# Selective attention and a gated feed-forward block on one core: the last 64 queries of batch 0 computed later, the bias of two heads added by matmuls, and loads moved between DMA queues

## The chip, the cores and the metric

The kernel runs on one core of one Trainium2 chip. The metric is device time in microseconds (us), lower is better. Timed runs give the median; a separate profiled execution gives the trace, whose times count from the start of its span.

## What is computed

The inputs are q, k, v of shape (8 batches, 8 heads, 576 positions, 64), s of shape (8, 8, 576), and three weight matrices. Per batch and head:

```
scores = q @ k.T / sqrt(64)
cum    = cumsum(max(s, 0))
scores = where(key > query, -1e9, scores + min(-(cum[query] - cum[key]), 0))
attn   = softmax(scores) @ v
```

Each batch's eight heads side by side are 576 rows of x (4608 rows of 512 in all). Then out = (silu(x @ w_gate) * (x @ w_val)) @ w_out, with 1536 inner columns. All inputs are float32; the kernel computes in bfloat16 with float32 sums.

## The kernel before

**Stages.** The 4608 rows are cut into nine feed-forward tiles of 512 rows (TT, NTT, lines 46 and 47). A batch has 576 rows, so tile 0 needs only the first 512 rows of batch 0, and the last 64 belong to tile 1. The kernel computes the whole attention of batch 0 first (first_batch, lines 882 to 925), and then runs a loop over the tiles (lines 952 to 969) in which attention of the later batches is interleaved with feed-forward products.

**Scores.** KQ holds the transposed keys and queries of four heads per buffer, two buffers in turn. In each of its tiles one 64-row half is data and the other half carries four extra rows with the cumulative sums, copied there from HL by small DMAs (aug, line 192). So one 128-row matmul gives product and bias together. HL is made on VectorE (DVE) from s by five operations (lines 236 to 242). score_piece (line 350) makes a head's scores in four pieces, 1600 columns in all; in batch 0 two pieces share one wide PSUM bank and one exponential on ScalarE (ACT), 1024 and 576 columns wide (line 388). There are two wide banks. GpSimd (POOL) then clears the positions above the diagonal with two selects (lines 391 and 396).

**Values and x.** av_piece (line 403) multiplies the exponentials with the values, 15 matmuls of 65 columns per head (the last column gives the row sum); av_out (line 421) divides on DVE; x_pe (line 456) transposes two heads' results on TensorE and ACT copies them into XT, the input of the feed-forward products.

**Start.** SP loads s, then k and q of the first eight heads (load_one, called load_qk for both), then after the four HL copies the values (load_v, line 166) and k and q of heads 8 to 11. The number given to load_qk is a group of four heads: 0 and 1 are batch 0, 2 and 3 batch 1. ACT casts group 0, TensorE transposes it in two 64-row halves (pe_transpose_half), and ACT and DVE copy it out of PSUM (pe_out). Weights come by w_load (line 331) on GpSimd's queue, with a cast to bfloat16: gate and value weights in two parts each (g0, v0, g1, v1), the output weights in two (o0, o1).

**Order in the loop.** Every engine executes its instructions in the order of the program. ffn_items yields after each unit of a tile: 24 for gate and value products (gate_value, lines 619 to 662: four 512-column matmuls, a tanh on ACT, DVE products), then those of the down product (lines 664 and 689). n counts units. After each unit the dictionary hook (line 945) may place something, and pump places attention steps of the next batch in proportion to n. In tile 0 pump begins at n = 6 (n0, line 958), and the transposes of group 2 (prep_one, line 529) stand at n = 1 to 4.

The softmax here doesn't subtract the row's maximum and nothing guards it: scores larger than these inputs give would overflow.

## Time and profile before

| | us |
|---|---|
| median of three timed runs | 383.56 (382.58 to 383.68) |
| profiled execution, its own time | 383.17 |
| span of its trace | 381.3 |
| TensorE busy in the span | 363.5 (95%) |
| DVE, ACT, POOL busy | 289.6, 242.7, 205.9 |
| first score matmul of batch 0 (line 375) starts | 11.15 |
| first feed-forward matmul (line 626) starts | 32.03 |
| weights of the first products land, g0 and v0 | 26.7 and 30.7 |
| tile 1's first feed-forward matmul starts | 79.81 |

So the profiled execution has 1.87 us outside its span. A matmul's row in the profile gives its start and a modelled end that includes the way through the array, so a stream of matmuls is priced by the distance between starts and not by the duration of one. Landing times are issue start plus the profile's time to landing.

### The profile page before, as it was taken

Reading aid. Unit: us, or ns where it says so; the run is one execution under the profiler, and the core shown is the slowest. Engines: PE = TensorE matmul, PEld = TensorE weight load, DVE = VectorE, ACT = ScalarE, POOL = GpSimd, SP = SyncE. Lnnn points to the kernel's source line nnn. Section 1 sums busy time; section 2 is a strip of 40 time slices with the busy share of each in tenths; the row PEclk is TensorE's granted clock in tenths of the full one; section 3 lists DMA queues with packets and bytes.
Section 4 is the critical chain, followed back from the end, with each engine's and each line's share of the span. In section 5 each row is a group of like instructions: output and inputs, shape, how many; then the busy total and the mean of one; then the engine's idle time right before and its main releaser. Section 6 shows DMA issues by size and latency. Waiting matters only on the chain. (4 is left out here: it accounts for less than half of the span.)

```text
span 381.3 us, 8674 instructions
## 1 busy us (share of the span) xinstructions
PE 363.5 (95%) x3246; PEld 230.5 (60%) x3246; DVE 289.6 (76%) x577; ACT 242.7 (64%) x459; POOL 205.9 (54%) x326
## 2 busy tenths in 40 slices
PE   3779999998999999999999999999999999999995
PEld 3666556655555555865586558655875575476464
DVE  8666787456895799868986899589958866975983
ACT  8586788676977786578767876697455523323321
POOL 6684357545364636595458647775665426315220
PEclk9999999999999999999999999999999999999999
DMA  7999999997477998498739965987223213002003
GB/s 234 197 253 263 198 242 268 348 259 162 163 167 246 236 285 220 105 287 216 194 114 285 270 149 158 252 179 166 37 80 101 32 19 127 0 2 97 14 2 110
DMA packets 100729, 64.22 MB, mean 168 GB/s; under 512 B 81888, under 2 KB 85824, under 8 KB 100688
## 3 DMA queue, kind: packets, MB, share of 16 engines
q1 hardware_dynamic: 91248, 46.15, 48.6%
q0 software_dynamic: 9440, 17.53, 17.7%
q8 instruction: 25, 0.41, 0.4%
q14 instruction: 16, 0.13, 0.1%
HBM read 37.90 MB, written 19.86 MB: 151 GB/s over the span
## 5 line engine op out<-in xcount | busy, mean ns | idle before, releaser
L388 ACT ACTIVATE pt<-bank 128x512 bf16<-128x512 f32 x224 | 106.7, 506 | 26.5 <-PE bank L375 18.3
L626 PE MATMUL bank<-XT,wg 128*128 128x512 bf16 x432 | 110.9, 379 | 0.6 <-DVE pp L633 0.2
L641 PE MATMUL bank<-XT,wv 128*128 128x512 bf16 x432 | 110.8, 379 | 0.2
L631 ACT ACTIVATE th<-bank 128x512 bf16<-128x512 f32 x108 | 64.7, 599 | 60.0 <-PE bank L626 54.7
L633 DVE SCALAR_TENSOR_TENSOR pp<-th,bank 128x512 bf16<-128x512 bf16 x108 | 73.9, 684 | 30.2 <-ACT th L631 29.5
L649 DVE SCALAR_TENSOR_TENSOR ht<-pp,bank 128x512 bf16<-128x512 bf16 x108 | 74.1, 686 | 10.3 <-POOL ht L658 0.5
L658 POOL TENSOR_TENSOR ht<-ht 128x512 bf16<-128x512 bf16 x35 | 40.4, 1154 | 53.9 <-DVE su L656 53.8
L375 PE MATMUL bank<-kq 128*128 128x128 bf16 (+4 forms) x504 | 67.5, 240 | 1.6 <-DVE kq L284 1.1
L375 PEld LDWEIGHTS <-kq 128*128 128x128 bf16 x576 | 46.7, 99 | 34.8 <-issue 5.7
L641 PEld LDWEIGHTS <-wv 128*128 128x128 bf16 x432 | 38.6, 98 | 35.8 <-issue 0.4
L626 PEld LDWEIGHTS <-wg 128*128 128x128 bf16 x432 | 38.5, 98 | 35.2 <-issue 1.2
L391 POOL TENSOR_SCALAR_AFFINE_SELECT pt<-pt 128x512 bf16<-128x512 bf16 x64 | 41.8, 653 | 28.5 <-ACT pt L388 28.1
L413 PEld LDWEIGHTS <-pt 128*128 128x128 bf16 x960 | 41.1, 98 | 16.0
L413 PE MATMUL bank<-vt,pt 128*128 128x65 bf16 x840 | 41.8, 194 | 0.0
L447 POOL DMA_DIRECT2D xs<-ot x24 | 21.9, 912 | 31.7 <-DVE ot L430 31.7
L711 PEld LDWEIGHTS <-ht 128*128 128x128 bf16 x336 | 31.2, 98 | 4.3
L197 POOL DMA_DIRECT2D kq<-HL x52 | 31.2, 602 | 0.1
L430 DVE TENSOR_TENSOR ot<-bank,rc 128x320 bf16<-128x320 f32 x56 | 27.5, 492 | 1.9
L396 POOL TENSOR_SCALAR_AFFINE_SELECT pt<-pt 128x64 bf16<-128x64 bf16 x64 | 16.7, 261 | 18.9 <-ACT pt L388 18.7
L711 PEld LDWEIGHTS <-su 128*128 128x128 bf16 x252 | 23.6, 98 | 3.3
L670 PE MATMUL bank<-wo,ht 128*128 128x512 bf16 x96 | 24.6, 379 | 0.0
L775 POOL TENSOR_TENSOR ysb<-ysb 128x512 f32<-128x512 f32 x12 | 15.2, 1271 | 15.3 <-DVE ysb L770 15.3
(96 smaller groups left out, 396.9 us busy)
## 6 DMA issues: line engine op xcount, KB each, us to landing
rawk<-in_k_dram SPq DMA_DIRECT2D x15, 576.0 KB
rawq<-in_q_dram SPq DMA_DIRECT2D x15, 576.0 KB
rawv<-in_v_dram SPq DMA_DIRECT2D x32, 256.0 KB
out_dram<-ysb POOLq DMA_DIRECT2D x32, 256.0 KB, 3.8
xs<-ot POOLq DMA_DIRECT2D x24, 160.0 KB, 3.7
ks<-ck SPq DMA_DIRECT2D x11, 288.0 KB
qs<-cq SPq DMA_DIRECT2D x11, 288.0 KB
wg<-in_moe_w_gate_dram POOLq DMA_DIRECT2D x2, 768.0 KB, 12.6
```

The lines of the kernel that those rows point to most:

```text
L197: engs[hh].dma_start(KQ[hb % 2][r][r0 : r0 + 4, :, e * S : (e + 1) * S], HL[bh : bh + 1, :, :, :],)
L375: nc.tensor.matmul(sc[:, o : o + w], T[:, 1, e * S + 128 * tj : e * S + 128 * (tj + 1)], T[:, 0, e * S + lo : e * S + hi], start=True, sto ...
L388: nc.scalar.activation(pt[:, c0 : c0 + W], sc[:, 0:W], AF.Exp, scale=0.125)
L391: nc.gpsimd.affine_select(pt[:, 1088:1600], pt[:, 1088:1600], pattern=[[0, 4], [1, 128]], compare_op=ALU.is_ge, fill=zreg, base=0, channel ...
L413: nc.tensor.matmul(av[:, bi * (D + 1) : (bi + 1) * (D + 1)], pt[:, c0 : c0 + 128], VT[b % 2][:, tj, h, :], start=(tj == 0), stop=(tj == bi),)
L626: nc.tensor.matmul(pg, WG[j][:, c, f0 : f0 + 128], xt[:, c, :], start=(c == 0), stop=(c == 3),)
L631: nc.scalar.activation(th, pg, AF.Tanh, scale=0.5)
L633: nc.vector.scalar_tensor_tensor(pp, in0=th, scalar=1.0, in1=pg, op0=ALU.add, op1=ALU.mult)
L641: nc.tensor.matmul(pv, WV[j][:, c, f0 : f0 + 128], xt[:, c, :], start=(c == 0), stop=(c == 3),)
L649: nc.vector.scalar_tensor_tensor(hp[:, 2 * k2 : 2 * k2 + 2, :].rearrange("p a n -> p (a n)"), in0=pp, scalar=0.5, in1=pv, op0=ALU.mult, op ...
L658: (nc.vector if ft == NFT - 1 else nc.gpsimd).tensor_sub(hp[:, 1:3, :], hp[:, 1:4:2, :], hp[:, 0:3:2, :])
L711: nc.tensor.matmul(ps, lhs(p), rhs(p), start=(first and p == 0), stop=(last and p == NP - 1), skip_group_check=True,)
```

## The change

Batch 0 is computed in two parts. first_batch goes. Its place takes a list written out by hand: score_first makes the first 512 queries of a head in two halves of 640 columns, each with one exponential; mask_first clears four diagonal blocks with one select; av_first uses 10 matmuls per head; x_first copies 512 columns. The last 64 queries (score_tail, av_tail, x_tail) stand in the hook of tile 0: the eight score_tail at n = 1 to 8, av_tail at 6 and 10, x_tail at 12. The transposes of group 2 move to n = 9 to 12 and n0 from 6 to 12.

For heads 0 and 1 score_first doesn't use the extra rows. HL now has 128 partitions: rows 64 to 71 repeat the first eight heads of s, loaded by a second DMA on ACT's queue after a memset on GpSimd. Two more matmuls per chunk add the bias, with a selection column (pick, made from the identity) against the rows of HL. The copies of HL's rows for heads 0 and 1 come later; those for heads 2 and 3 go on GpSimd's queue.

The loads of groups 2 and 3 go on GpSimd's queue, the values of batch 0 come in three steps on SP's, w_load calls move, 32 warm-up matmuls (keep_warm) stand at the start, one large memset moves from DVE to GpSimd, and a few casts and copies out of PSUM change engine (k of group 0's second half goes from ACT to DVE, q of group 1's first half from DVE to ACT, the cast of group 1's k from DVE to GpSimd). The loop over the later tiles, pump and the feed-forward code are otherwise the same.

```diff
--- before.py
+++ after.py
@@ -95,15 +95,16 @@
-    HL = const.tile([BH, 4, 2, S], BF16)
+    HL = const.tile([128, 4, 2, S], BF16)
...
-    s_sb = first.tile([BH, S], FP32)
-    c8 = first.tile([BH, S], FP32)
+    s_sb = first.tile([128, S], FP32)
+    c8 = first.tile([128, S], FP32)
+    pick = first.tile([128, 2, 2], BF16)
...
-        def load_one(hb, name, rs=(0, NR)):
+        def load_one(hb, name, rs=(0, NR), eng=nc.sync):
...
-            nc.sync.dma_start(
+            eng.dma_start(
...
-        nc.sync.dma_start(s_sb, s.rearrange("b h n -> (b h) n"))
-        def init_vt(i):
-            nc.gpsimd.memset(VT[i][:, :, :, D : D + 1], 1.0)
-            nc.gpsimd.memset(VT[i][64:128, 4, :, 0:D], 0.0)
+        flat = s.rearrange("b h n -> (b h) n")
+        nc.sync.dma_start(s_sb[0:BH], flat)
+        nc.gpsimd.memset(s_sb[64:128], 0.0)
+        nc.scalar.dma_start(s_sb[64 : 64 + H], flat[0:H])
+
+        def init_vt(i, eng):
+            eng.memset(VT[i][:, :, :, D : D + 1], 1.0)
+            eng.memset(VT[i][64:128, 4, :, 0:D], 0.0)
 
...
+        nc.vector.tensor_add(pick[:, 0, :], ident[:, 0:2], ident[:, 64:66])
+        nc.vector.tensor_scalar(pick[:, 1, :], pick[:, 0, :], -1.0, None, ALU.mult)
...
-        init_vt(0)
-        init_vt(1)
-        nc.vector.memset(aug_rows(1, 0), 0.0)
+        nc.gpsimd.memset(aug_rows(1, 0), 0.0)
         nc.gpsimd.memset(aug_rows(1, 1), 0.0)
         pads(1)
+        init_vt(0, nc.vector)
...
-            c8, one_s[0:BH, 0:1].to_broadcast([BH, S]), s_sb, 0.0, ALU.mult, ALU.add
+            c8, one_s[:, 0:1].to_broadcast([128, S]), s_sb, 0.0, ALU.mult, ALU.add
...
-        nc.vector.tensor_copy(HL[:, 2:4, 0, :], HL[:, 0:2, 1, :])
+        nc.vector.tensor_copy(HL[64:128, 0, 1, :], HL[64:128, 1, 1, :])
+        nc.vector.tensor_copy(HL[0:64, 2:4, 0, :], HL[0:64, 0:2, 1, :])
...
+        W1 = 640
+        FIRST_CHUNKS = [
+            [(0, 0, 384), (1, 128, 256), (1, 256, 384)],
+            [(0, 384, 512), (2, 256, 512), (1, 384, 512), (3, 384, 512)],
+        ]
...
+        def score_first(bh, half):
+            hb, hh = divmod(bh, HB)
+            if half == 0:
+                pts[bh] = PTP[0].tile([128, 2 * W1], BF16, tag="pt", bufs=8, name="pt")
+            r, e = divmod(hh, 2)
+            T = KQ[hb % 2][r]
+            bs = take("w")
+            sc = view(bs, 1024)
+            o = 0
+            for (tj, lo, hi) in FIRST_CHUNKS[half]:
+                keys = slice(128 * tj, 128 * (tj + 1))
+                lhs = T[:, 1, e * S + keys.start : e * S + keys.stop]
+                rhs = T[:, 0, e * S + lo : e * S + hi]
+                out_s = sc[:, o : o + hi - lo]
+                o += hi - lo
+                if bh > 1:
+                    nc.tensor.matmul(out_s, lhs, rhs, start=True, stop=True)
+                    continue
+                nc.tensor.matmul(out_s, lhs[0:64], rhs[0:64], start=True, stop=False)
+                nc.tensor.matmul(
+                    out_s, HL[:, 0, 1, keys], pick[:, 0, bh : bh + 1].to_broadcast([128, hi - lo]),
+                    start=False, stop=False,
+                )
+                nc.tensor.matmul(
+                    out_s, pick[:, 1, bh : bh + 1].to_broadcast([128, 128]), HL[:, 0, 1, lo:hi],
+                    start=False, stop=True,
+                )
+            nc.scalar.activation(
+                pts[bh][:, half * W1 : (half + 1) * W1], sc[:, 0:W1], AF.Exp, scale=0.125
+            )
+            give(bs)
+
+        def mask_first(bh):
+            m = pts[bh].rearrange("p (b n) -> p b n", n=128)[:, 0:10:3, :]
+            nc.gpsimd.affine_select(
+                m, m, pattern=[[0, 4], [1, 128]],
+                compare_op=ALU.is_ge, fill=zreg, base=0, channel_multiplier=-1,
+            )
+
+        def av_first(h):
...
+            for bi in range(4):
+                for tj in range(bi + 1):
+                    c0 = first_col(tj, bi)
+                    nc.tensor.matmul(
+                        av[:, bi * (D + 1) : (bi + 1) * (D + 1)],
+                        pts[h][:, c0 : c0 + 128],
+                        VT[0][:, tj, h, :],
+                        start=(tj == 0),
+                        stop=(tj == bi),
+                    )
...
+        def x_first(pr):
+            ot = ots.pop(pr)
+            bs = take()
+            ps = view16(bs, 512)
+            for c in range(4):
+                nc.tensor.transpose(ps[:, c * 128 : (c + 1) * 128], ot[:, c, :], ident)
+            nc.scalar.copy(XT[:, pr, 0:512], ps)
...
+        def score_tail(bh):
+            hb, hh = divmod(bh, HB)
+            pr, e2 = divmod(bh, 2)
+            if e2 == 0:
+                tls[pr] = PTP[0].tile([128, 3, TT // 2], BF16, tag="su", bufs=NFT // 2, name="su")
+            r, e = divmod(hh, 2)
+            T = KQ[hb % 2][r]
+            bs = take()
+            sc = view(bs, NCH * 64)
+            for tj in range(NCH):
+                nc.tensor.matmul(
+                    sc[:, tj * 64 : (tj + 1) * 64],
+                    T[:, 1, e * S + 128 * tj : e * S + 128 * (tj + 1)],
+                    T[:, 0, e * S + 512 : e * S + S],
+                    start=True,
+                    stop=True,
+                )
+            tl = tail_view(pr)
+            nc.scalar.activation(
+                tl[:, e2].rearrange("p c n -> p (c n)"), sc, AF.Exp, scale=0.125
+            )
...
+        def av_tail(g):
+            if g == 0:
...
+            for i in range(4):
+                h = 4 * g + i
+                tl = tail_view(h // 2)
+                for tj in range(NCH):
+                    nc.tensor.matmul(
+                        av[0:64, i * (D + 1) : (i + 1) * (D + 1)],
+                        tl[:, h % 2, tj, :],
+                        VT[0][:, tj, h, :],
+                        start=(tj == 0),
+                        stop=(tj == NCH - 1),
+                    )
...
+        def x_tail():
...
+            for pr in range(4):
+                nc.tensor.transpose(
+                    ps[:, pr * 64 : (pr + 1) * 64], ot[0:64, pr, :], ident[0:64, 0:64]
+                )
+            nc.scalar.copy(
+                XT[:, :, 512:576], ps.rearrange("p (a n) -> p a n", a=4)
+            )
...
+        def keep_warm(n):
+            bs = take()
...
+        keep_warm(32)
...
-        aug(0, SP4)
-        load_v(0, range(5))
-        load_qk(2)
+        def aug_one(hh, eng):
+            r, e = divmod(hh, 2)
+            r0 = 64 * (1 - r)
+            eng.dma_start(
+                KQ[0][r][r0 : r0 + 4, :, e * S : (e + 1) * S], HL[hh : hh + 1, :, :, :]
+            )
+
+        load_v(0, (0, 1))
+        aug_one(2, nc.gpsimd)
+        aug_one(3, nc.gpsimd)
+        aug(1, SP4)
+        load_v(0, (2, 3))
...
-        aug(1, GP4)
-        for nm, eng in (("k", nc.scalar), ("q", nc.vector)):
+        w_load("g", 0)
...
-                pe_out(0, nm, g, 1, eng)
-        cast_one(1, "k", nc.vector)
...
+        score_first(0, 0)
+        score_first(0, 1)
+        aug_one(0, nc.sync)
+        second_rows("k")
+        score_first(1, 0)
+        second_rows("q")
+        score_first(1, 1)
+        aug_one(1, nc.sync)
+        load_v(0, (4,))
+        cast_one(1, "k", nc.gpsimd)
+        w_load("v", 0)
         cast_one(1, "q", nc.vector)
-
...
-            wq = {1: (("g", 0), ("v", 0)), 4: (("g", 1),), 5: (("v", 1),)}
-            tail = {
-                6: ("a0", "a1"),
-                7: ("a2", "a3", "a4", "x0", "a5", "x1", "a6", "a7", "x2", "w6", "x3", "w8"),
-            }
-            for h in range(H):
-                for ci in range(4):
...
-                        pe_transpose(1, nm, g)
-                    for r in range(2):
-                        for nm, g in order:
-                            pe_out(1, nm, g, r, nc.vector)
-                    for c in range(3, 5):
...
-                    aug(2, SP4)
-                if h == 7:
-                    aug(3, SP4)
-                    load_qk(3)
-                    load_v(1, range(5))
-                    load_qk(4)
-                    cast_one(2, "k", nc.gpsimd)
-                    cast_one(2, "q", nc.gpsimd)
-                    load_qk(5)
-                    w_load("o", 0)
-                    w_load("o", 1)
...
-        first_batch()
+        cast_v(0, 0, nc.gpsimd)
+        cast_v(0, 1, nc.gpsimd)
+        mask_first(0)
+        score_first(2, 0)
+        score_first(2, 1)
+        for g in range(2):
+            pe_transpose(1, "k", g)
+            pe_out(1, "k", g, 0, nc.vector)
+        mask_first(1)
+        score_first(3, 0)
+        for g in range(2):
+            pe_transpose(1, "q", g)
+        score_first(3, 1)
+        cast_v(0, 2, nc.gpsimd)
+        cast_v(0, 3, nc.gpsimd)
+        mask_first(2)
+        for g in range(2):
+            pe_out(1, "q", g, 0, nc.scalar)
+        for nm in ("k", "q"):
+            for g in range(2):
+                pe_out(1, nm, g, 1, nc.vector)
+        mask_first(3)
+        score_first(4, 0)
+        score_first(4, 1)
+        mask_first(4)
+        for nm in ("k", "q"):
+            load_one(2, nm, eng=nc.gpsimd)
+        av_first(0)
+        score_first(5, 0)
+        av_first(1)
+        score_first(5, 1)
+        mask_first(5)
+        av_first(2)
+        score_first(6, 0)
+        av_first(3)
+        score_first(6, 1)
+        mask_first(6)
+        w_load("g", 1)
+        av_first(4)
+        score_first(7, 0)
+        av_first(5)
+        score_first(7, 1)
+        mask_first(7)
+        cast_v(0, 4, nc.gpsimd)
+        x_first(0)
+        av_first(6)
+        x_first(1)
+        keep_warm(6)
+        av_first(7)
+        x_first(2)
+        keep_warm(8)
+        x_first(3)
+        keep_warm(8)
         second_psum()
         first_sbuf.close()
         PTP[0] = ctx.enter_context(tc.tile_pool(name="later", bufs=1))
-        PTP["bufs"] = 5
...
-        hook = {
-            1: [lambda: prep_one(2, 0)],
-            2: [lambda: prep_one(2, 1)],
-            3: [lambda: prep_one(2, 2)],
-            4: [lambda: prep_one(2, 3)],
-            6: [lambda: cast_one(3, "k", nc.gpsimd), lambda: cast_one(3, "q", nc.gpsimd)],
-        }
+        hook = {n: [] for n in range(1, 37)}
+        for bh in range(H):
+            hook[1 + bh].append(lambda bh=bh: score_tail(bh))
+        hook[1].append(lambda: w_load("v", 1))
+        hook[4].append(lambda: aug(2, SP4))
+        hook[4].append(lambda: [load_one(3, nm, eng=nc.gpsimd) for nm in ("k", "q")])
+        hook[6].append(lambda: cast_one(2, "k", nc.gpsimd))
+        hook[6].append(lambda: av_tail(0))
+        hook[7].append(lambda: cast_one(2, "q", nc.gpsimd))
+        hook[8].append(lambda: aug(3, SP4))
+        hook[8].append(lambda: load_v(1, range(5)))
+        hook[9].append(lambda: init_vt(1, nc.gpsimd))
+        hook[10].append(lambda: av_tail(1))
+        hook[12].append(x_tail)
+        for i in range(4):
+            hook[9 + i].append(lambda i=i: prep_one(2, i))
+        hook[11].append(lambda: w_load("o", 0))
+        hook[14].append(lambda: [cast_one(3, nm, nc.gpsimd) for nm in ("k", "q")])
+        hook[14].append(lambda: load_qk(4))
+        hook[15].append(lambda: w_load("o", 1))
+        hook[20].append(lambda: load_qk(5))
...
-            n0 = 6 if tt == 0 else 0
+            n0 = 12 if tt == 0 else 0
```

## The prediction

> **What bounds the kernel now.** The chain of waits covers only the last microsecond here, so it says nothing of the rest. I read first the shares of the span and the 40 slices, from the page:
>
> ```profile
> PE 363.5 (95%) x3246; PEld 230.5 (60%) x3246; DVE 289.6 (76%) x577; ACT 242.7 (64%) x459; POOL 205.9 (54%) x326
> ...
> PE   3779999998999999999999999999999999999995
> PEld 3666556655555555865586558655875575476464
> DVE  8666787456895799868986899589958866975983
> ACT  8586788676977786578767876697455523323321
> ```
>
> TensorE (PE) is full in every slice but the first three or four. So there are two regimes: the attention of batch 0, before the first feed-forward matmul, and a long stretch in which TensorE's stream sets the end. Busy time in 10-us stretches confirms the second (PE, PEld, DVE, ACT, POOL, clock, DMA share, GB/s):
>
> ```profile
> 32.00:42.00 10.00, 9.55 (x69) 5.40 (x70) 7.71 (x12) 7.23 (x13) 3.16 (x4) 1.00 1.14 244
> 42.00:52.00 10.00, 9.91 (x69) 5.33 (x68) 8.01 (x12) 8.73 (x18) 2.68 (x6) 1.00 1.21 208
> 52.00:62.00 10.00, 10.00 (x107) 6.13 (x106) 6.38 (x13) 7.34 (x15) 8.63 (x15) 1.00 0.99 305
> 62.00:72.00 10.00, 10.00 (x131) 6.62 (x128) 7.85 (x17) 8.63 (x17) 5.25 (x12) 1.00 0.94 258
> ```
>
> From 32 us on the reader sees almost no room on PE: what is added there is paid in full, and the tiles start as early as batch 0 lets them. Batch 0 itself, from the timeline (start, duration, engine, what, and in brackets the wait before it):
>
> ```profile
> 11.15 1.51 PE L375 MATMUL wide<-kq 128*128 128x128 bf16 x9 [0.57 <-DMA kq<-HL]
> ...
> 12.22 1.56 ACT L388 ACTIVATE pt<-wide 128x1024 bf16<-128x1024 f32 x2 [1.98 <-PE wide L375]
> ...
> 17.26 10.13 ACT L388 ACTIVATE pt<-wide 128x1024 bf16<-128x1024 f32 x12 [1.35 <-PE wide L375]
> ...
> 18.34 0.95 PE L375 MATMUL wide<-kq 128*128 128x128 bf16 x9 [0.86 <-ACT pt L388]
> ...
> 31.97 0.58 PEld L626 LDWEIGHTS <-wg 128*128 128x128 bf16 x4 [0.29 <-issue]
> ```
>
> Heads 0 and 1 wait for TensorE; the exponentials of heads 2 to 7 then run back to back until 27.39; from there 4.6 us of masks, value products, division, transposes and copies lead to the first product.
>
> **What the skill says.** "TensorE: Matmul & The Clock Gate", Part 1: the array runs at half rate until about 3.4 us of sustained work have released its clock. The trace agrees: the nine matmuls of 1600 columns take 1.51 us at 11.15 and 0.95 at 18.34, and five transposes at 14.60 still take 0.72 where five at 32.89 take 0.44. Same page, "LDWEIGHTS" and "Weight-path perf modes": loading weights costs their columns over 1.2 GHz, and the fast load needs all 128 columns. No row of before shows 64-column weights at full rate. "DMA: Bandwidth & Descriptors", "Queues, rings and completion order": each DMA engine takes turns between queues packet by packet, so a queue of small packets gets few bytes beside one of large packets. The trace agrees: SP needed 24 us to issue four value loads (256 KB each) while the weights came down GpSimd's queue:
>
> ```profile
> 28.35 24.09 SPq L172 DMA_DIRECT2D rawv<-in_v_dram  x4
> ```
>
> **The change, part by part.**
>
> (1) *Start.* ACT's first instruction becomes a DMA that waits for a memset of 64x576 on POOL (the 64x608 row takes 0.60), so it issues near 1.4 and takes about 0.6 like SP's. Table load (1.28) and two fills (2.45) follow, and the first cast moves from 4.69 to 5.95. On DVE the five HL operations took 3.60 to 7.82. They now wait for the second copy of s: 3.6 if it lands at once, 4.8 if it needs the 3.4 us that the slowest HL copy needed; I take 4.0. A further copy costs half of the 0.45 row. HL is ready at 8.5, the q copies behind it on DVE (1.44) end at 9.9. The HL DMA that head 0 waited for is off the path, so the first score starts at 9.9 instead of 11.15: 1.25 gained.
>
> (2) *Heads 0 and 1.* Each chunk has three matmuls for one: 640 x 3 = 1920 columns per half, four halves. At half rate (0.83 ns a column) a half is 1.6 us, at full rate 0.8. With the two transposes of the second rows (0.96 each at half rate) that is 8.3 us of PE; if the clock rises near 15 us, 7.1, so head 1's last half ends at 17.0. The q copies on DVE, queued behind, end at 17.4, and head 2's exponential starts at about 17.9 where it started at 17.26. The gain of (1) is spent.
>
> (3) *Heads 2 to 7.* An exponential of 640 columns is 0.70 (between 644 ns for 576 and 1024 ns for 1024); before, a head took 10.13 / 6 = 1.69, now 1.24 (overlapping, as 1.56 for the pair of 1.67 shows) to 1.40, so 7.9 for six, plus 1.46 for the two q copies of group 1 (750 and 710 ns) now on ACT between heads 3 and 4, plus some 0.9 of waits around them. The last ends at 17.9 + 7.9 + 1.5 + 0.9 = 28.2, before 27.39. Mask selects (0.65 each, eight for sixteen), two loads and the weight issue (0.8 each) on POOL lie beside it; the value casts for chunks 2 and 3 stand ahead of mask 2 and hold every later mask if their data is late (rival C).
>
> (4) *After the last exponential*: mask 0.65, ten matmuls at 31 ns (30 value matmuls from 24.26 to the next score at 25.19) and 0.2 of way, 0.19 + 0.43 on DVE, transposes 0.4, copy 0.58, handovers 0.35: 2.9 for 4.6. Six of eight value products now lie between scores. First product at **31.1**, against 32.03: **0.9 gained**.
>
> (5) *Tails on PE.* 40 score matmuls of 64 columns: 31 ns each, 1.25. 40 value matmuls with 64-column weights: 31 to 53 ns (the second the skill's price, an estimate), 1.25 to 2.1. Four transposes, 0.2. Sum 2.7 to 3.6; below that only if they fill gaps that are there now (0.45 in the stretch from 32 to 42). I take 3.1. Eight exponentials (320 columns, about 0.45 each), four selects, DVE divisions and a copy hide beside it: ACT has 2.8 of 10 us free in that stretch, DVE 2.3.
>
> (6) *Order in tile 0.* Attention of batch 1 is pressed from 30 units into 24. ACT: six tanh 3.6, eight heads at 1.75 = 14.0, q and k copies, casts and output copies about 7.6, so 25 in some 32 us of PE. It fits. The values of batch 1, issued at n = 8 behind weights on the other queue, cost 0 (if they land by about 58) to 3. The group-3 casts stand on POOL just ahead of the transposes at n = 14: 0 to 0.8. Before had a comparable pause (PE idle around 41). I take 0.4 for both.
>
> (7) *Loads.* g0 and v0 are issued about 5 us earlier; 6.7 MB (groups 0 and 1, values, g0, v0) at the some 300 GB/s of 11 to 31 us are in by about 25, so the products don't wait. The moved memsets end on POOL at about 6.4, before their users: nothing.
>
> Sum on the profiled execution: 383.17 - 0.9 + 3.1 + 0.4 = 385.8 (span 383.9 and 1.87 around it). The median before is 0.4 above the profiled one: **386.1**.
>
> **Rivals.**
>
> A, above: tails cost more than the start saves, 385 to 387.5. For it: PE full from 32 us. Chance 0.43.
>
> B, near no change: the 32 warm-up matmuls (3.4 us at half rate, from 2.1 to 5.5) release the clock before the first score. Then (2) takes 4 us, DVE's copies set the pace, and the same sums give 29.1 for the first product: 2.9 gained, 3.1 + 0.4 paid, 384.2. Against it: before, PE was busy for 3.88 and 3.80 of the 5-us stretches from 5 and from 10 without being released. Chance 0.22.
>
> C, slower still: the value loads of batch 0's chunks 2 and 3 are issued at about 11.5, when g0 starts on the other queue. At the 49 GB/s of the 24-us issue (1.18 MB) they would need up to 10.7 us, land near 22, and through POOL's order put the first product at 32.3; with 1.5 lost on batch 1's values, 388.5 to 389. Chance 0.15.
>
> D, faster: the clock as in B, ready by 10 us, and the tails at their lower price of 2.7 with 0.9 of it in pauses that tile 0 has now. 383.6 - 3.2 + 1.8 = 382.2. It decides in favour once the first product starts before 29.0. For it: two unknowns of one sign suffice. Chance 0.20.
>
> **How the numbers follow.** About 0.3% (1.15 us) can be told from no change. Slower: A, C: 0.43 + 0.15, and a little of B: 0.61. Same: the rest of B: 0.20. Faster: D and a remainder: 0.19. The range reaches from D's to C's time and leaves both far ends out: 381.8 to 389.0. The time is A's.
>
> **What would show it.** Right: first score near 9.9, first product at 30.5 to 31.7, tile 1's first product about 2.5 later than before, 80 short matmuls for the tails at 31 to 53 ns from start to start. B and D: score matmuls of heads 0 and 1 at 53 ns per 128 columns. C: POOL waiting for value data before its casts. The prediction is wrong if the first product starts before 29 or TensorE shows no added length in tile 0.

## The result, and the profile after

| | before | after |
|---|---|---|
| median of four timed runs, us | 383.07 | 400.28 (397.90 to 401.29) |
| ratio to before, 95% interval | | 1.044 (1.039 to 1.050) |
| profiled execution, its span | 383.17, 381.3 | 397.90, 396.0 |
| first score of batch 0 | 11.15 | 9.96 |
| head 2's first exponential | 17.26 | 22.41 |
| last exponential of batch 0 ends | 27.39 | 34.19 |
| first feed-forward product | 32.03 | 37.45 |
| tile 0: from there to tile 1's first product | 47.78 | 56.78 |
| from there to the end of the span | 301.5 | 301.8 |

The change makes the kernel 4.4% slower. The profiled execution has 14.7 us more span: 5.4 before the first product, 9.0 in tile 0, 0.3 in all the rest. The forecast had -0.9, +3.5 and 0, so it missed 6.3 us at the start and 5.5 in tile 0. The profiled execution is the fastest of the four runs; what made the others 1.4 to 3.4 us slower stands in no trace, so all that follows explains the 14.7 us.

From the page of the kernel after, the busy time of TensorE and its 40 slices, with those of ScalarE:

```profile
PE 374.4 (95%) x3297; PEld 237.3 (60%) x3338; DVE 290.1 (73%) x582; ACT 243.3 (61%) x468; POOL 209.6 (53%) x327
...
PE   5979979899899999999999999999999999999995
...
ACT  7266669488697688657875787578556522322321
```

The share of busy time is the same 95%; only the slices show that the full stretch starts later and has holes in slices 6 and 8, which are tile 0. Batch 0 from the timeline of the kernel after (start, duration, engine, what, and in brackets the wait before it):

```profile
9.96 0.47 PE L384 MATMUL wide<-kq 64*128 64x384 bf16 x1 [1.21 <-DVE kq L333]
...
18.20 0.70 ACT L393 ACTIVATE pt<-wide 128x640 bf16<-128x640 f32 x1 [2.68 <-PE wide L389]
21.80 1.30 ACT L393 ACTIVATE pt<-wide 128x640 bf16<-128x640 f32 x2 [2.90 <-PE wide L389]
...
27.56 0.78 PE L382 MATMUL wide<-kq 128*128 128x384 bf16 x7 [2.02 <-ACT kq L331]
...
37.45 1.02 PE L775 MATMUL bank<-XT,wg 128*128 128x512 bf16 x3 [0.23 <-ACT XT L438]
```

The first score comes 1.2 us earlier, as forecast. Then ScalarE waits for TensorE before each exponential of heads 0 and 1, 1.8 to 3.0 us, where the kernel before waited up to 2.0. Head 4 waits another 2.0 us for the copies of q, which stand on ScalarE behind the exponentials of head 3.

Tile 0 in stretches of 10 us (PE, PEld, DVE, ACT, POOL, clock, DMA share, GB/s; the clock is the share of its full rate that TensorE was granted), and some of TensorE's waits in the whole span (us in total, times, longest):

```profile
47.00:57.00 10.00, 7.71 (x72) 4.23 (x71) 8.08 (x13) 6.56 (x13) 3.39 (x7) 1.00 1.07 209
57.00:67.00 10.00, 8.92 (x68) 5.27 (x71) 5.29 (x8) 8.76 (x17) 4.49 (x8) 1.00 1.02 215
...
77.00:87.00 10.00, 8.13 (x103) 5.48 (x102) 6.07 (x13) 9.68 (x18) 3.59 (x8) 1.00 1.01 280
```

```profile
...
PE wide L382 <- ACT kq L331: 2.0, 1, 2.0
PE bank L304 <- POOL ck L263: 1.9, 1, 1.9
PE bank L819 <- ACT pt L537: 1.5, 1, 1.5
...
PE bank L528 <- DVE kq L333: 0.9, 1, 0.9
```

TensorE was almost full from 32 us on before (it lacked 0.45 us in the first 10 us); now it lacks 2.3, 1.1 and 1.9 us in three stretches. Two of the waits name their cause: the transposes of group 3 wait for GpSimd's cast, which stands behind the mask selects of head 8 and runs at 56.27; and near 79 the exponentials stand on ScalarE behind its cast of group 5, which waited 3.0 us for its load.

### The profile page after: what moved, and what is told of

It is laid out like the page before. It is cut to its first block, busy times and chain, and to the rows that moved or that the text cites. A ratio compares the mean times of both kernels' runs of the same rounds, so it can differ in the third digit from the quotient of the medians.

```text
span 396.0 us, 8844 instructions
## 1 busy us (share of the span) xinstructions
PE 374.4 (95%) x3297; PEld 237.3 (60%) x3338; DVE 290.1 (73%) x582; ACT 243.3 (61%) x468; POOL 209.6 (53%) x327
## 5 line engine op out<-in xcount | busy, mean ns | idle before, releaser
L775 PE MATMUL bank<-XT,wg 128*128 128x512 bf16 x416 | 109.4, 379 | 1.8 <-DVE kq L333 0.5
L790 PE MATMUL bank<-XT,wv 128*128 128x512 bf16 x414 | 109.6, 379 | 1.5 <-DVE kq L333 0.3
L528 PEld LDWEIGHTS <-kq 128*128 128x128 bf16 x504 | 40.5, 98 | 28.6 <-issue 1.8
L540 POOL TENSOR_SCALAR_AFFINE_SELECT pt<-pt 128x512 bf16<-128x512 bf16 x56 | 36.7, 655 | 30.5 <-ACT pt L537 30.2
L562 PEld LDWEIGHTS <-pt 128*128 128x128 bf16 x840 | 37.1, 98 | 15.8
L198 POOL DMA_DIRECT2D kq<-HL x48 | 28.7, 600 | 0.0
L819 PE MATMUL bank<-wo,ht 128*128 128x512 bf16 x89 | 23.8, 379 | 1.8 <-ACT pt L537 1.5
L545 POOL TENSOR_SCALAR_AFFINE_SELECT pt<-pt 128x64 bf16<-128x64 bf16 x56 | 14.6, 261 | 18.7 <-ACT pt L537 18.6
```

Source lines behind the costliest of these rows:

```text
L198: engs[hh].dma_start(KQ[hb % 2][r][r0 : r0 + 4, :, e * S : (e + 1) * S], HL[bh : bh + 1, :, :, :],)
L528: nc.tensor.matmul(sc[:, o : o + w], T[:, 1, e * S + 128 * tj : e * S + 128 * (tj + 1)], T[:, 0, e * S + lo : e * S + hi], start=True, sto ...
L540: nc.gpsimd.affine_select(pt[:, 1088:1600], pt[:, 1088:1600], pattern=[[0, 4], [1, 128]], compare_op=ALU.is_ge, fill=zreg, base=0, channel ...
L562: nc.tensor.matmul(av[:, bi * (D + 1) : (bi + 1) * (D + 1)], pt[:, c0 : c0 + 128], VT[b % 2][:, tj, h, :], start=(tj == 0), stop=(tj == bi),)
L775: nc.tensor.matmul(pg, WG[j][:, c, f0 : f0 + 128], xt[:, c, :], start=(c == 0), stop=(c == 3),)
L790: nc.tensor.matmul(pv, WV[j][:, c, f0 : f0 + 128], xt[:, c, :], start=(c == 0), stop=(c == 3),)
```

## The experiments

My theory was that four losses lie side by side: the bias in place, its half clock, the tails' own work, and the order in tile 0. Below, "first product" and "tile 0" are read from each run's trace as in the table above; the kernel after ran a second time beside the second four, as r_after. A ratio compares with runs of the kernel before made beside that experiment.

### First four: one part each

**e1_rows**: heads 0 and 1 with the extra rows again.

```diff
-                if bh > 1:
+                if bh >= 0:
...
+        aug_one(0, nc.sync)
+        aug_one(1, nc.sync)
         aug_one(2, nc.gpsimd)
...
-        aug_one(0, nc.sync)
...
-        aug_one(1, nc.sync)
```

> Heads 0 and 1 get their bias from the extra rows again (one matmul per chunk), all else as in the changed kernel. Theory T (four separate losses; the bias in place costs some 4 to 5 us of the start): first score near 11.5 instead of 9.96, because it waits for the row copies again; head 2's first exponential near 17.5 instead of 22.4; first product at 32 to 33.5 instead of 37.45; total 395 to 396.5. Rival R1 (the late start comes from the value loads or from the exponentials, not from the three matmuls): first product stays above 36, total 399 or more.

Measured: 396.26, ratio 1.035 (1.031 to 1.039). The first score came at 13.61, since the row copies stood on SP behind two value loads, and not at 11.5; head 2's first score still came at 18.82 instead of 21.56, and the first product at 36.0. The three matmuls cost more than the 3.65 us by which they start earlier. But of the 2.7 us at head 2 only 1.4 arrived at the first product, about a third of what the theory gave it: neither the theory's 33.5 at most nor clearly rival R1's 36 or more.

**e2_full**: the same three matmuls, all of 128 rows.

```diff
-                nc.tensor.matmul(out_s, lhs[0:64], rhs[0:64], start=True, stop=False)
+                nc.tensor.matmul(out_s, lhs, rhs, start=True, stop=False)
```

> The bias of heads 0 and 1 stays in place, but the product runs over all 128 rows (its extra rows are zero then), so that the three matmuls of a chunk have the same number of rows. Theory S (of the cost of the bias in place, some 0.2 us per chunk, 14 chunks, comes from switching between 64 and 128 rows, where the weights are not loaded ahead): a 128-column chunk at half rate takes 0.33 instead of 0.545; head 2's first exponential near 19.8; first product 34.7 to 35.5; total 397.5 to 398.5. Rival (three times the columns at half rate are the whole cost): chunk still 0.5, nothing moves by more than 0.5, total 400.

Measured: 396.11, ratio 1.033 (1.032 to 1.035). A chunk of 128 columns at half rate took 0.32 instead of 0.545 (in the kernel after, 11.66 to 12.20), as theory S said, and the clock came up at 12.85 instead of 24.65:

```profile
10.88 0.31 PE L384 MATMUL wide<-kq 128*128 128x128 bf16 x1
10.99 0.31 PE L385 MATMUL wide<-pick,HL 128*128 128x128 bf16 x1
11.10 0.31 PE L389 MATMUL wide<-HL,pick 128*128 128x128 bf16 x1
11.20 0.31 PE L384 MATMUL wide<-kq 128*128 128x128 bf16 x1
```

Head 2's first score: 16.66 instead of 21.56. But of the 4.9 us at head 2 only 2.0 arrived at the first product (35.44). TensorE's and GpSimd's waits in this kernel show why:

```profile
PE one L411 <- POOL vt L184: 4.0, 2, 3.1
```

```profile
POOL vt L184 <- DMA rawv<-in_v_dram: 7.2, 2, 6.6
```

The values of chunks 2 and 3 are late; this is rival C's mechanism. In the kernel after GpSimd waited for the same data (1.7 us), but TensorE got there later still.

**e3_no_tail**: no tails; it leaves out the last 64 queries of batch 0 and puts zeros in their place.

```diff
-            hook[1 + bh].append(lambda bh=bh: score_tail(bh))
+            pass
...
-        hook[6].append(lambda: av_tail(0))
...
-        hook[10].append(lambda: av_tail(1))
-        hook[12].append(x_tail)
+        hook[12].append(lambda: nc.gpsimd.memset(XT[:, :, 512:576], 0.0))
```

> Leaves out the last 64 queries of batch 0 (scores, values and transposes of the tails; zeros stand in their place). Theory T: the tails cost their matmuls, 2.9 us, in tile 0 and nothing else much: tile 0 from first product to tile 1's first product 53 to 54 instead of 56.6, total 396.5 to 397.5. Rival R2 (the tails' exponentials on ScalarE and their banks are what stalls tile 0): the stalls go too, tile 0 at 48 to 49, total 391.5 to 393.

Measured: 394.42, ratio 1.029 (1.028 to 1.031); tile 0 took 53.64 instead of 56.78 (57.20 in the second run of the kernel after). So 3.1 to 3.6 us go, and both long waits in tile 0 stay, at 1.9 and 0.9 (a third, for DVE's copies, grows from 0.9 to 1.4). The tails' 84 matmuls hold TensorE for 3.0 to 3.2 us in the two traces of the kernel after, counted from each group's first start to the next other matmul: they cost their matmuls and little else. The median fell by more than the trace explains, as the runs of the kernel after spread over 3.4 us; against r_after's 398.11, below, it fell by 3.7.

**e45_order**: two lines of the hook.

```diff
-        hook[14].append(lambda: [cast_one(3, nm, nc.gpsimd) for nm in ("k", "q")])
+        hook[12].append(lambda: [cast_one(3, nm, nc.gpsimd) for nm in ("k", "q")])
...
-        hook[20].append(lambda: load_qk(5))
+        hook[14].append(lambda: load_qk(5))
```

> Two lines of the hook move: the casts of group 3 from n = 14 to 12 (ahead of the mask selects on GpSimd), the load of group 5 from n = 20 to 14 (ahead of other loads on SP). Theory T (order in tile 0 costs some 6 us of pauses, of which the wait for GpSimd's cast is 1.9 to 2.3 and the wait behind ScalarE's cast of group 5 is 1.5): both waits go, tile 0 at 53 to 54 instead of 56.6, total 396.5 to 397.5. Rival R3 (the pauses are one backlog that shows up wherever the order lets it; taking two away makes two others longer): tile 0 stays at 55.5 or more, total 399.5 to 400.5.

Measured: 393.70, ratio 1.027 (1.025 to 1.029); tile 0 took 52.53, 4.25 less. Both waits are gone, and the stretches are full again:

```profile
47.00:57.00 10.00, 9.09 (x87) 5.31 (x87) 8.28 (x14) 7.57 (x14) 4.95 (x9) 1.00 1.04 210
...
77.00:87.00 10.00, 9.89 (x125) 6.58 (x125) 5.98 (x12) 7.92 (x16) 6.06 (x13) 1.00 1.17 299
```

Two lines of order are worth more than all of the tails' matmuls. Rival R3, one backlog that moves elsewhere, falls.

### Second four: what keeps the start late

**r_after**: the kernel after, unaltered.

> The changed kernel unaltered, beside the others on one chip, since its runs lay 3.4 us apart. Theory: 398 to 401; first product near 37.4 in the profile.

Measured: 398.11, ratio 1.039 (1.038 to 1.041), first product 37.34.

**e6_vals**: e2_full, and

```diff
-        load_v(0, (0, 1))
+        load_v(0, range(4))
...
         aug(1, SP4)
-        load_v(0, (2, 3))
```

> As e2_full (bias in place, all matmuls of 128 rows), and the four full value loads of batch 0 are issued on SP ahead of the row copies of heads 4 to 7, not two before and two after. Theory V (with the row switch gone, the values of chunks 2 and 3 are what is late: TensorE waited 3.1 and 0.9 us for GpSimd's casts of them, and its clock fell meanwhile): these two waits go, first product at 31.5 to 33 instead of 35.44, total 392 to 393.5. Rival (the row copies of heads 4 to 7, now later, or the copies out of PSUM take over): first product stays at 34.5 or later, total 395 or more.

Measured: 394.76, ratio 1.031 (1.029 to 1.034), first product 33.59, between the two expectations. TensorE's wait for values is gone, but head 4's first score now waits for its row copies until 23.82:

```profile
PE wide L382 <- DMA kq<-HL: 4.5, 1, 4.5
```

GpSimd still waited 4.6 us for chunk 3. Swapping loads on one queue moved the lateness from one to the other.

**e7_warm**: 36 idle matmuls in TensorE's pause.

```diff
+        keep_warm(36)
         score_first(4, 0)
```

> The changed kernel with 36 idle matmuls ahead of head 4's scores, where TensorE stands still for 2.0 us (25.5 to 27.5). Theory K (the pause drops the granted clock to half from 28.3 to 31.5, and heads 4 to 6 are bound by TensorE then): no clock of 0.5 after it, score and value matmuls of heads 4 to 6 at full rate, first product at 35.7 to 36.3 instead of 37.45, total 1.2 to 1.7 less than r_after. Rival (the clock falls for another reason, or the exponentials set the pace anyway): clock still at 0.5 near 29, or first product within 0.4 of 37.45, total as r_after.

Measured: 397.79, ratio 1.041 (1.037 to 1.044); first product 37.49. No gain. The clock stayed up after this filler, and the way from head 4's first score to the first product fell from 9.89 to 9.21; but the filler ran from 26.16 to 28.3, and head 4 started at 28.28 instead of 27.56. So the half clock after the pause costs 0.7 us, not the 1.5 I gave it. This run shows something else. The record of the clock (the column after POOL) starts at its first change and reads 1.00 until then whatever the rate. Here it starts with a rise at 5.96, before heads 0 and 1, so that it covers them:

```profile
12.00:16.00 4.00, 4.00 (x24) 1.98 (x23) 0.43 (x1) 1.41 (x2) 3.60 (x6) 0.50 0.93 120
16.00:20.00 4.00, 4.00 (x22) 1.86 (x21) 2.16 (x4) 0.70 (x1) 0.24 (x1) 0.50 1.16 211
20.00:24.00 4.00, 3.74 (x25) 2.45 (x25) 1.28 (x3) 2.00 (x3) 0.63 (x1) 0.50 1.18 219
```

TensorE counts as busy for 11.7 of 12 us and yet stays at half clock. In e2_full, with the same number of matmuls, all of 128 rows:

```profile
12.00:16.00 4.00, 4.00 (x48) 3.20 (x46) 2.33 (x4) 1.88 (x3) 3.81 (x6) 0.89 0.93 126
16.00:20.00 4.00, 2.72 (x37) 2.22 (x35) 3.52 (x5) 3.48 (x6) 0.81 (x1) 1.00 1.16 208
```

The number of weight loads in 4 us doubles, and the clock is up after 3 us. In both runs it had fallen just before the first score, at 9.37 and 9.43.

**e8_all**: the edits of e6_vals, e7_warm and e45_order together.

> The four repairs together: all matmuls of 128 rows, values ahead of the row copies, 36 idle matmuls ahead of head 4, casts of group 3 at n = 12 and load of group 5 at n = 14. The tails stay. Theory T (separate losses that add up): first product at 30.5 to 31.5, tile 0 at 52 to 53, total 385.5 to 387. Rival (one loss hides behind another, so that repairing all brings less than the sum): 389 or more.

Measured: 388.80, ratio 1.017 (1.014 to 1.020), 9.3 less than the kernel after beside it. This lies between the two expectations. Tile 0 took 52.33 as expected, the first product came at 32.71 instead of 30.5 to 31.5: the filler itself waited 1.0 for a bank, ran until 23.5, and held head 4 up.

### Third four: the start mended, and what is left

**e9_start**: e6_vals, with g0 and v0 later and the copies of q earlier.

```diff
-        w_load("g", 0)
...
-        w_load("v", 0)
...
         mask_first(0)
+        w_load("g", 0)
+        w_load("v", 0)
...
             pe_transpose(1, "q", g)
+        pe_out(1, "q", 0, 0, nc.vector)
+        pe_out(1, "q", 1, 0, nc.scalar)
         score_first(3, 1)
...
-            pe_out(1, "q", g, 0, nc.scalar)
```

> On e6_vals, two more edits in the start alone: the weight loads g0 and v0 are issued after mask 0 (near 16 us, as the kernel before had them) instead of at 11.4 and 13.3, and the copies of q of group 1 out of PSUM stand ahead of head 3's second half, one on VectorE and one on ScalarE. Theory B (since g0 and v0 came first on the other queue, the values of chunk 3 and the row copies of heads 4 to 7 crawl in beside them at some 200 GB/s until 23.8, and after that the way from head 4's score to the first product is 9.2 us whatever the clock): score of head 4 at 20.5 to 21.5 instead of 23.8, first product at 29.8 to 30.8, tile 0 at 56 to 57 as before the edit, total 389.5 to 391.5. Rival (the loads are late for want of queue order on SP, not for the weights): head 4 waits until 22.5 or later again, first product at 32.5 or later, total 393 or more.

Measured: 390.66, ratio 1.021 (1.019 to 1.023). Head 4's first score at 21.07, first product at 30.29, tile 0 at 56.16: as expected. GpSimd's wait for values fell from 4.6 us to one of 0.55, and the wait for the row copies is gone: the weights were what both crawled beside. What the order of the copies of q adds to head 4's start was not tried apart.

**e10_prep**: e9_start and e45_order, and group 2 three units earlier.

```diff
-        hook[6].append(lambda: cast_one(2, "k", nc.gpsimd))
+        hook[2].append(lambda: cast_one(2, "k", nc.gpsimd))
...
-        hook[7].append(lambda: cast_one(2, "q", nc.gpsimd))
+        hook[3].append(lambda: cast_one(2, "q", nc.gpsimd))
...
-            hook[9 + i].append(lambda i=i: prep_one(2, i))
+            hook[6 + i].append(lambda i=i: prep_one(2, i))
```

> e9_start with the two edits of e45_order, and the preparation of group 2 three units earlier (casts at n = 2 and 3, transposes at n = 6 to 9). Theory T: beside the tails' own matmuls, tile 0 then holds no pause of over 0.6 us, 50.8 to 51.6 from first product to tile 1's, the 47.8 of before plus the predicted 3.1 and some 0.4; total 384 to 385.5. Rival (attention squeezed into 24 units costs pauses wherever it stands): tile 0 stays at 52.3 or more, total 386 or more.

Measured: 386.50, ratio 1.010 (1.009 to 1.012); first product 29.85, tile 0 53.01. Tile 0 is a miss, and by its numbers the rival's case (52.3 or more, 386 or more). But the new order made a wait of its own, the tails' transposes behind a division that stands on DVE behind copies of q:

```profile
PE bank L507 <- DVE ot L495: 1.2, 1, 1.2
```

**e11_no_tail**: e10_prep with the edit of e3_no_tail; it too leaves out the last 64 queries of batch 0.

> e10_prep without the tails: leaves out the last 64 queries of batch 0 (zeros in their place). Theory T (with the order mended the tails cost their matmuls and nothing else): 2.8 to 3.2 us less than e10_prep, all of it in tile 0, total 381 to 382.5. Rival (their exponentials and banks cost as much again): 4.5 or more less.

Measured: 382.97, ratio 1.000 (0.999 to 1.001); tile 0 49.56, 3.45 less than e10_prep, which has that 1.2 us wait among it. Without its last 64 queries the mended kernel is just level with the kernel before: a first product 1.8 us earlier, a tile 0 that is 1.8 us longer. Of these, 1.5 are pauses of TensorE (2.0 us in tile 0, against 0.5 before); that they come from batch 1's attention being pressed into fewer units is likely, but not shown.

**e12_before_warm**: the kernel before, with

```diff
+        keep_warm(36)
         cast_half(0, "k", 0, nc.scalar)
...
```

> The kernel before with 36 warm-up matmuls at its start and nothing else. If they release the clock by head 0's scores: nine score matmuls near 11.15 take 0.95 instead of 1.51, head 2's exponential starts 0.8 to 1.3 earlier than 17.26, and the total is 0.8 to 1.3 under the kernel before. Rival (they stop just short of the release, as in the changed kernel, whose transposes at 6.6 still ran at half rate): transposes at 1.17, no change.

Measured: 383.52, ratio 1.003 (1.002 to 1.004). The clock was up at 5.4 (nine transposes in 0.69), but TensorE then waited 1.3 for a cast and 0.9 for the next, and from 9.19 the transposes took 1.17 again. The first score came at 11.90, 0.75 later. Neither expectation held. The cast of q on ScalarE waited 1.3 for its load, against 0.2 in the kernel before; why that load came later stays open.

### Last three: the two open terms

**e13_grouped**: the kernel after, with the products of a half first and then its bias matmuls, which run in a second loop over the same chunks.

```diff
-                    continue
-                nc.tensor.matmul(out_s, lhs[0:64], rhs[0:64], start=True, stop=False)
+                else:
+                    nc.tensor.matmul(
+                        out_s, lhs[0:64], rhs[0:64], start=True, stop=False, skip_group_check=True
+                    )
+            o = 0
+            for (tj, lo, hi) in FIRST_CHUNKS[half] if bh < 2 else ():
...
```

> The changed kernel with another order within each half of heads 0 and 1: all products of 64 rows first, then all bias matmuls of 128 rows, so 2 changes of the row count for each half instead of 6 or 8. Theory S (the change of the row count costs some 0.2 us for each chunk): a half of three chunks takes 1.8 to 1.95 from first score to the exponential instead of 2.35, the clock comes up earlier, first product some 1.5 to 2.5 earlier than 37.4. Rival (a matmul of 64 rows is slow by itself): no change, a half still 2.3.

Measured: 395.81, ratio 1.032 (1.028 to 1.036); first product 35.10, 2.3 earlier, and the first half took 1.91 to its exponential, both as theory S said. The kernel after, one chunk with its weight loads (PEld), and this kernel's first half:

```profile
11.66 0.10 PEld L384 LDWEIGHTS <-kq 64*128 64x128 bf16 x1 [0.20 <-issue]
11.66 0.29 PE L384 MATMUL wide<-kq 64*128 64x128 bf16 x1
11.88 0.11 PEld L385 LDWEIGHTS <-HL 128*128 128x128 bf16 x1
11.88 0.29 PE L385 MATMUL wide<-pick,HL 128*128 128x128 bf16 x1
11.89 0.12 PEld L389 LDWEIGHTS <-pick 128*128 128x128 bf16 x1
11.96 0.31 PE L389 MATMUL wide<-HL,pick 128*128 128x128 bf16 x1
12.20 0.10 PEld L384 LDWEIGHTS <-kq 64*128 64x128 bf16 x1 [0.20 <-issue]
```

```profile
9.96 0.69 PE L384 MATMUL wide<-kq 64*128 64x384 bf16 x3 [2.07 <-DVE kq L333]
10.58 0.50 PE L392 MATMUL wide<-pick,HL 128*128 128x384 bf16 x1
...
11.41 0.31 PE L392 MATMUL wide<-pick,HL 128*128 128x128 bf16 x1
11.52 0.31 PE L396 MATMUL wide<-HL,pick 128*128 128x128 bf16 x1
```

In the first fence a weight load begins together with its own matmul wherever the rows change, 0.22 us after the matmul before started on the way from 64 to 128 rows and 0.24 on the way back, against 0.08 between two of 128 rows. In the second, three products of 64 rows take 0.62 for 640 columns, which is half rate (0.53) and little else. So it is the change of rows that costs, not the 64-row matmul. The Trainium skill has a rule that fits: "TensorEngine Tiling (Array Packing)", "Key Properties", says that changing the tiling mode drains TensorE. It gives no price, and doesn't say whether a plain matmul on 64 of the 128 rows is such a change; the traces show the price, not the drain.

**e14_spread**: e10_prep, with

```diff
-        hook[12].append(x_tail)
+        hook[16].append(x_tail)
...
-        hook[12].append(lambda: [cast_one(3, nm, nc.gpsimd) for nm in ("k", "q")])
+        hook[9].append(lambda: [cast_one(3, nm, nc.gpsimd) for nm in ("k", "q")])
...
-            n0 = 12 if tt == 0 else 0
+            n0 = 9 if tt == 0 else 0
```

> e10_prep with the tails' transposes at n = 16 instead of 12, pump from n = 9 instead of 12, and the casts of group 3 at n = 9. Theory (the 1.7 us that tile 0 is over the forecast are the 1.2 that the transposes waited for their division and the pressed attention): tile 0 at 51.0 to 51.8, total 384.7 to 385.5. Rival (the tails cost more than their matmuls): 52.5 or more, total as e10_prep, 386.5.

Measured: 385.39, ratio 1.006 (1.004 to 1.007); tile 0 51.64, as the theory said. TensorE's pauses in tile 0 fell from 2.5 us in e10_prep to 1.4, so most of the rest of tile 0's excess was order too; which of the three edits did it was not tried apart. This is the best version of the change that I found, still 0.6% slower than the kernel before.

**e15_rows**: e10_prep with the edit of e1_rows, the row copies of heads 0 and 1 ahead of the value loads.

> e10_prep with the bias of heads 0 and 1 from the extra rows (their two row copies first on SP), one matmul per chunk. Theory (once the switches are gone, the bias in place starts 1.2 us earlier and spends about as much on three times the columns): within 0.7 of e10_prep's 386.5. Rivals: the extra rows are better by 1 us or more, or the row copies land as late as in e1_rows (13.6) and it is 1 us or more worse.

Measured: 386.48, ratio 1.007 (1.005 to 1.009), within the theory's 0.7; first product 30.1 against 29.85 in e10_prep. With its switches mended, the bias in place is worth nothing that can be measured: it starts 1.2 us earlier (9.97 against 11.18) and spends that on its columns.

## Why the prediction was wrong

The direction was right, but for the most part by luck. A's reason was that the tails cost more than the start saves. The tails cost what A said, 3.1 to 3.6 of the 14.7 us. The start saved nothing and lost 5.4, and most of what tile 0 lost was a term of 0.4. By the prediction's own steps:

| step | forecast | kernel after | |
|---|---|---|---|
| (1) first score | 9.9 | 9.96 | right |
| (2) head 2's first exponential | 17.9 | 22.41 | 4.5 missed |
| (3) from there to the last exponential's end | 10.3 | 11.8 | 1.5 missed |
| (4) from there to the first product | 2.9 | 3.3 | 0.4 missed |
| (5) tails | 3.1 | 3.1 to 3.6 | right |
| (6) order in tile 0 | 0.4 | about 5.5 | 5.1 missed |
| (7) weights | in time | g0 19.0, v0 24.1 | right for them |

**Step (2) failed** in "1920 columns per half ... At half rate (0.83 ns a column) a half is 1.6 us". Columns were priced, changes of shape were not. Each of the 14 chunks has two changes of the row count, some 0.22 us together (0.545 against 0.32 in e2_full), so 3.1 us. And "if the clock rises near 15 us" failed with it: it rose at 24.65. In all five profiled runs with these switches it stayed down from the first score until 24.3 to 26.4, 2.9 us or more after the last switch; in all eight kernels that keep the bias in place with no switches or fewer it was up between 12.9 and 15.8. In all these traces the clock changed only at the ends of windows of 3.41 us (last section). 14 windows of the five runs began at half clock, counted as busy throughout with the switches among their work, and ended without a rise (where the record of the clock doesn't reach, by the durations of the matmuls). The other 17 windows that began at half clock and counted as busy throughout, one of them with the grouped order of e13_grouped, all ended with a rise. So the alternation is what keeps the clock down; that it does so because TensorE drains is argued from this, not shown apart. The slow first halves before 15 us were in the forecast; the two later ones and the transposes at half rate are the other 1.2 or so.

**Step (3)** put some 0.9 for waits. The exponentials took the 7.9 that it gave them and the copies of q 1.3, but ScalarE waited 2.5 in between. TensorE stood still for 2.0 us behind the copies of q, and the half clock after that pause cost 0.7 (e7_warm). **Step (4)** adds up to 3.1 from its own terms, not 2.9, and so missed 0.2 rather than 0.4.

**Step (6)** was the largest. The text looked at ScalarE's sum of work (25 us in 32) and found that it fits. A sum says nothing of an order: the casts of group 3 were named ("stand on POOL just ahead of the transposes at n = 14: 0 to 0.8") but not what stands ahead of them on POOL, two mask selects, the first of which waited 6.1 us for exponentials; the load of group 5 at n = 20, with its cast on ScalarE ahead of exponentials, was not priced at all. e45_order gave 4.25 back, and e14_spread, in a kernel whose start is mended too, came to 51.64, where the forecast had 47.8 + 3.5 = 51.3.

**Step (7)** came out, though two of its readings did not: from 11 to 31 us the trace of before shows 226 GB/s and not some 300, and the 24 us of rival C's 49 GB/s belong to the last four of five value loads, while 1.18 MB is all five (24.55 us, 48 GB/s). Neither changes the result; nor does the chance of "faster", 0.19, that is less than D's own 0.20.

**The rivals.** B's clock release failed in the profiled execution (transposes at 6.62 still took 1.17); in others, such as e2_full and e7_warm, it came (0.69), and was lost again during the 2-us pause before the first score. C's late values were real, but in the kernel after they lay in the shadow of step (2), and came out when that was mended (3.1 and 0.9 us in e2_full). D needed B's clock and tails of 2.7 with 0.9 of that in pauses; neither came. The range failed because all its cases shared two prices, the column price in (2) and the small sum in (6).

With the order mended and the switches gone, e14_spread and e10_prep ran in 385.4 and 386.5, near the forecast of 386.1, and A's reason holds in e14_spread: the start saves 1.6 and tile 0 costs 3.9. So the sum priced a kernel in which only the work itself costs something. But these kernels also load in another order than the change does, so they don't test the sum of its steps one by one.

## What to carry to other kernels

Price a matmul stream by its changes of shape as well as by its columns: alternating 64-row and 128-row matmuls cost 0.2 us for each chunk here and kept the clock down; put equal shapes side by side or fill up the rows. For a step that moves in an in-order program, list what stands ahead of it on each engine and what that waits for; an engine's sum of work against the time there is hides just the waits that decide. When one wait is mended, look for the next one in its shadow: the values, then the row copies, then the weights on the other queue came out one after another.

## What was not expected of the hardware

- The release of the clock at the start is a matter of chance: after 32 or 36 warm-up matmuls of 3.3 to 3.6 us in all, the transposes 1 us later take 0.69 in some kernels and 1.17 in others that are the same up to there. "TensorE: Matmul & The Clock Gate", Part 1, in the Trainium skill, says that the window which decides runs freely, so that the point varies from run to run; this agrees. In the clock records of all 17 traces every stretch of one clock but the last lasts a whole multiple of 3.41 us, so in each run the clock changed only at points of a grid, which lies differently from run to run. In the eight runs with a grid point 2.9 to 4.0 us after the first warm-up matmul the clock rose there; in the eight whose points lie up to 2.6 us and from 4.4 us after it, it didn't.
- Pauses well under a window of 3.41 us were enough to lose the clock. The same section gives about 3.4 us of idle time; the measurement is shorter. In e2_full TensorE was idle from 7.9 to 9.97, and the clock fell at 9.43. In e9_start no pause in the window before the fall was longer than 1.2 us (start and end of the window, its length, busy time of TensorE and the other engines, clock, DMA):

```profile
4.98:8.40 3.42, 1.68 (x25) 1.30 (x22) 3.27 (x6) 3.42 (x6) 1.48 (x3) 1.00 0.90 292
8.40:11.81 3.41, 1.84 (x12) 1.43 (x13) 1.51 (x3) 0.64 (x3) 2.40 (x4) 0.50 1.15 326
11.81:15.22 3.41, 3.41 (x24) 2.41 (x22) 1.11 (x2) 1.36 (x2) 2.86 (x5) 0.50 1.14 196
15.22:18.64 3.42, 3.02 (x40) 2.43 (x39) 2.58 (x4) 1.84 (x3) 1.73 (x3) 1.00 0.69 70
```

All 16 falls in the first 375 us of the 17 traces came at the end of a window in which TensorE counted as busy for half of it or less; every window at full clock busy for less than 0.44 of it ended with a fall, and none busy for more than 0.50 did. Between the two both occur, so the busy time of the profile, in which the ends of matmuls are modelled, is not the whole rule.

- Tail value matmuls with 64-column weights: 33 ns from start to start (20 of them at 43.60 in the kernel after), near the lower end of the 31 to 53 of the forecast.
